# A leaky ReLU taken from SBUF instead of PSUM, and three buffers for the raw weights of a later layer, in a fused attention and mixture-of-experts kernel

## The chip, the cores and the metric

The kernel runs on one core of a Trainium2 chip. Its time is the device time of one execution in microseconds (us). Three runs of the kernel before took 1252.9, 1254.32 and 1254.36 us, so its time is the median, 1254.32 us. The engines are named as in the profile: PE is TensorE (PEld its weight loads), DVE is VectorE, ACT is ScalarE, POOL is GpSimd, and SP is SyncE, which issues most of the DMAs (SPq is its queue).

## The reference

Three layers follow one another; nothing goes back to the host in between.

```python
# 1. attention between x (8, 8, 512, 64) and a state (8, 8, 32, 64), both ways
a  = softmax(x @ state.T / 8);   xread = a  @ state
a2 = softmax(state @ x.T / 8);   sread = a2 @ x
x  = concat([xread, sread])                 # 8 * 544 = 4352 tokens of 512
# 2. a dense layer with a leaky ReLU
h = x @ w_in                                # 512 -> 2048
g = np.maximum(0.01 * h, h)
x = g @ w_out                               # 2048 -> 512
# 3. eight experts, one per token
e   = argmax(x @ w_gate)
out = gate_w * eom[e] * (np.maximum(x @ w1[e], 0) @ w2[e])   # w1: 512 x 1024, w2: 1024 x 512
```

## The kernel before

**Stages.** The kernel has two long phases. In the first, tokens go through attention and the dense layer in nine chunks: one for each batch element (512 tokens), and a last one of 256 tokens for `sread` of all of them. A chunk has 16 steps, one for each 128 columns of `w_in`. Step n runs `mm1(n)`, which makes `h` (128 x 512 in one PSUM bank), and two steps later (`DEPTH` is 2) `mm2(n)`, which multiplies the result with `w_out` into four other banks. In the second phase 37 slots of 128 tokens go through the experts.

**Precision.** Products that need fp32 accuracy are made of high and low parts: `gh` is u rounded to a shorter format (by ACT), `gl` is what is left (by DVE), and three matmuls stand for one.

**The activation, in `mm1`.** The bank `h` is read twice: ACT (L721) writes 0.01 * h into the SBUF tile `u`, and DVE (L722) takes the maximum of the bank and `u`. ACT then rounds `u` to `gh` (L197), and DVE subtracts (`gl`, L198, called in the next step before that step's `mm1`). The bank comes from the pool `psa`, which has four banks for everything but `mm2`: `h`, the bank `kps` in which k is made, the attention's banks, and the small sums `tot`.

**Work that runs beside the steps.** The lists of each engine are in the order of the program text, so a step's lines say what is queued behind what.

- In steps 0 to 14 `w_in` and `w_out` arrive as raw 64-bit numbers and are turned into fp32 (`from_double`): ACT L179 and L180, DVE L183 and L187, and POOL L190, and for `w_out` the split into `woh` (ACT L193) and `wol` (POOL L194). Tiles `wor` (raw `w_out`) come from the pool `ps_p`.
- From step 14 on, the generator `presplit` scales the experts' weights and splits them into two fp16 parts, in 32 jobs of two halves of 512 KB. A job has four parts, between its `yield`s: squares of half 0 (ACT L97), squares of half 1, then the sum over partitions on PE (`tot`, L139), the scale and `halve` of half 0, and last `halve` of half 1. `halve` is DVE L627 and L628 and POOL L629. SP writes each result to DRAM (L655, L636). One part runs in each step, and in chunk 7 from its third step on two parts, so that jobs 25 to 31 take two steps each.
- The raw halves come from the same pool `ps_p`, with two buffers. From job 25 on (`SPARE`), two of three jobs use the attention's tiles `x` and `xT` instead, which are free by then, and are loaded two jobs ahead (`ahead`).
- The attention of the next chunk and the router of the chunk before run one part in each step too.

Of the kernel before, what the change touches and what calls it, by code (L numbers as in the profile page):

```python
# [9 lines left out]
FP32 = mybir.dt.float32  # L10
FP32R = mybir.dt.float32r
# [3 lines left out]
ACTF = mybir.ActivationFunctionType  # L15
ALU = mybir.AluOpType
# [7 lines left out]
def tile_attention_moe_moe2(ctx, tc, x, state, w_in, w_out, w_gate, w_ogate, w1, w2, out):  # L24
    nc = tc.nc
    B, H, S, D = x.shape
    NS = state.shape[2]
    DM, FF = w_in.shape
    w_in, w_out = w_in.bitcast(I32), w_out.bitcast(I32)
    E, _, F2 = w1.shape  # L30
    NTOK = out.shape[0]
    TB = S + NS
    HP = H // 2
    G = 2
    R = S // 128
    KD = DM // 128
    NF = FF // 128
    KF = F2 // 128
# [4 lines left out]
    scale = 1.0 / float(D) ** 0.5  # L43
# [37 lines left out]
                                   op=ALU.arith_shift_right)  # L81
    nc.vector.tensor_copy(tqf, tq)
    for t in range(NSR // 128):
        nc.vector.scalar_tensor_tensor(out=toks[:, t:t + 1], in0=tqf, scalar=float(TB - NS),
                                       in1=pidx_f, op0=ALU.mult, op1=ALU.add)
        nc.vector.tensor_single_scalar(out=toks[:, t:t + 1], in_=toks[:, t:t + 1],
                                       scalar=float(t * (128 // NS) * TB + S), op=ALU.add)
# [5 lines left out]
    def squares(o, t):  # L93

        k, n = t.shape[1:]
        with nc.allow_low_precision(reason="of the sum only the exponent is used"):
            nc.scalar.activation(out=junk[:, 0:k * n].rearrange("p (k n) -> p k n", n=n), in_=t, func=ACTF.Square,  # L97
                                 scale=2.0 ** 0.5, accum_out=o)

    def norm_scale(pool, ss, s, inv):  # L100

        u = pool.tile(list(ss.shape), I32, tag=f"u{ss.shape[1]}", name="u")
        nc.vector.tensor_single_scalar(out=u, in_=ss.bitcast(I32), scalar=24, op=ALU.arith_shift_right)
        nc.vector.tensor_scalar(out=s.bitcast(I32), in0=u, scalar1=-float(1 << 23),
                                scalar2=float(205 << 23), op0=ALU.mult, op1=ALU.add)
        nc.vector.tensor_scalar(out=inv.bitcast(I32), in0=u, scalar1=float(1 << 23),
                                scalar2=float(49 << 23), op0=ALU.mult, op1=ALU.add)
# [27 lines left out]
    def over_partitions(*cols):  # L135

        ps = psa.tile([128, cols[0].shape[1]], FP32, tag="a", name="tot")
        for i, t in enumerate(cols):
            nc.tensor.matmul(ps, ones16.bitcast(BF16), t, start=(i == 0), stop=(i == len(cols) - 1))  # L139
        return ps  # L140
# [16 lines left out]
    x_p = ctx.enter_context(tc.tile_pool(name="x", bufs=1))  # L157
# [3 lines left out]
    ab = ExitStack()  # L161
# [3 lines left out]
    at1 = ab.enter_context(tc.tile_pool(name="at1", bufs=1))  # L165
# [30 lines left out]
    def split_later(h, l, t):  # L196
        nc.scalar.copy(out=h, in_=t)  # L197
        return lambda: nc.vector.tensor_tensor(out=l, in0=t, in1=h.bitcast(FP32), op=ALU.subtract)  # L198
# [189 lines left out]
    wo_p = ab.enter_context(tc.tile_pool(name="wo", bufs=1))  # L388
    k_p = ab.enter_context(tc.tile_pool(name="kp", bufs=2))
    g_p = ab.enter_context(tc.tile_pool(name="gp", bufs=2))  # L390
    ps_p = ab.enter_context(tc.tile_pool(name="pre", bufs=2))
    pq_p = ab.enter_context(tc.tile_pool(name="preq", bufs=2))

    woh = [wo_p.tile([128, DM], FP32R, name=f"woh{f}") for f in range(NF)]
# [13 lines left out]
    def stage_wi():  # L408
        i = len(wi_raw)
        if i < len(pieces):  # L410
            fc, kh = pieces[i]
            raw = r_p.tile([128, KD // 2, FC, 2], I32, tag="y", name="wir")
            nc.sync.dma_start(
                raw.rearrange("p k f t -> p k (f t)"),
                w_in[kh * 256:(kh + 1) * 256, 2 * fc * FC:2 * (fc + 1) * FC].rearrange("(k p) f -> p k f", p=128))
            wi_raw.append(raw)
# [175 lines left out]
    def presplit():  # L592

        jobs = [(e, half, m) for e in range(E) for half in range(2) for m in range(2)]

        SPARE = (NF * (B - 1) - NF + 2) // 4 + 1
        spare = {}

        def load(n, i):
            if n >= len(jobs) or (n, i) in spare:  # L600
                return spare.pop((n, i), None)
            e, half, m = jobs[n]
            k = (n - SPARE + 1) % 3 if n >= SPARE else 0
            shape = [128, KD, F2 // 4] if m == 0 else [128, KF // 4, DM]
            if k == 0:
                t = ps_p.tile(shape, FP32, tag="raw", name="raw")
            else:
                if i == 0:
                    room = x_p.tile([128, R, H, D], FP32, tag="x", name="x") if k == 1 else \
                        at1.tile([128, HP, R, 128], FP32, tag="xT", name="xT")  # L610
                    spare[n] = room.rearrange("p a b c -> p (a b c)").rearrange("p (i k f) -> p i k f", i=2, k=shape[1])
                t = spare[n][:, i]
            q = slice((2 * half + i) * 256, (2 * half + i + 1) * 256)
            if m == 0:
                nc.sync.dma_start(t, w1[e, :, q].rearrange("(k p) f -> p k f", p=128))
            else:
                nc.sync.dma_start(t, w2[e, q].rearrange("(k p) d -> p k d", p=128))
            return t

        def ahead(n):  # L620
            if n < len(jobs):
                t = load(n, 0), load(n, 1)
                spare[n, 0], spare[n, 1] = t

        def halve(t, s):
            pc = pq_p.tile([128, 2] + list(t.shape[1:]), FP16, tag="pc", name="pc")
            nc.vector.tensor_scalar(out=pc[:, 0], in0=t, scalar1=s, scalar2=None, op0=ALU.mult)  # L627
            nc.vector.tensor_scalar(out=t, in0=t, scalar1=s, scalar2=None, op0=ALU.mult)  # L628
            nc.gpsimd.tensor_tensor(out=pc[:, 1], in0=t, in1=pc[:, 0], op=ALU.subtract)  # L629
            return pc  # L630

        t0, last = load(0, 0), None
        for n, (e, half, m) in enumerate(jobs):
            wd = w1d if m == 0 else w2d
            if last is not None:
                nc.sync.dma_start(*last)  # L636
            t1 = load(n, 1)
            if n >= SPARE:
                ahead(n + 2)
            ss = sm.tile([128, 2], BF16, tag="ss2w", name="ss2w")  # L640
            squares(ss[:, 0:1], t0)
            yield
            squares(ss[:, 1:2], t1)
            yield
            sa = sm.tile([128, 1], FP32, tag="saw", name="saw")
            s = esc[:, m, half, e:e + 1]
            nc.vector.tensor_scalar(out=sa, in0=over_partitions(ss[:, 0:1], ss[:, 1:2]), scalar1=128.0, scalar2=2.0 ** -94,
                                    op0=ALU.mult, op1=ALU.max)
            norm_scale(sm, sa, s, einv[:, m, half, e:e + 1])
            pc = halve(t0, s)  # L650
            if n == SPARE - 1:
                ahead(n + 1)
                ahead(n + 2)
            yield
            nc.sync.dma_start(wd[e, :, 2 * half], pc)  # L655
            t0 = load(n + 1, 0)
            last = wd[e, :, 2 * half + 1], halve(t1, s)
            yield
        nc.sync.dma_start(*last)

# [22 lines left out]
    pre = presplit()  # L683
# [12 lines left out]
    DEPTH = 2  # L696
# [3 lines left out]
    def mm1(n):  # L700
        c, f, gi, i, gf = steps[n]
        kind, b = chunks[c]
        T = S if kind == "x" else NSR
        later = []
        if i == 0 and c > 0:
            if kind == "x" or f == 0:
                later.append(k_make(gi + 1))
            if kind == "s":
                later.append(k_make(gi + 2))
        mh, ml = (a1h[b], a1l[b]) if kind == "x" else (srh, srl)  # L710
        ps = psa.tile([128, T], FP32, tag="a", name="h")
        kt = KT[kind]
        sl = slice(i * 128, (i + 1) * 128)
        for k in range(kt):
            nc.tensor.matmul(ps, k_h[gi][:, k, sl], mh[k], start=(k == 0), stop=False)
            nc.tensor.matmul(ps, k_h[gi][:, k, sl], ml[k], start=False, stop=False)
            nc.tensor.matmul(ps, k_l[gi][:, k, sl], mh[k], start=False, stop=(k == kt - 1))  # L717
        if i == 1 and c == 0:
            later.append(k_make(gi + 1))
        u = g_p.tile([128, T], FP32, tag="u", name="u")  # L720
        nc.scalar.activation(out=u, in_=ps, func=ACTF.Copy, scale=0.01)  # L721
        nc.vector.tensor_tensor(out=u, in0=ps, in1=u, op=ALU.max)  # L722
        gh = g_p.tile([128, T], FP32R, tag="gh", name="gh", bufs=DEPTH + 1)
        gl = g_p.tile([128, T], FP32R, tag="gl", name="gl", bufs=DEPTH + 1)
        for f in later:
            f()
        gt[n] = (gh, gl)
        return lambda: split_later(gh, gl, u)
# [30 lines left out]
    load_x(0)  # L759
    for _ in range(2):  # L760
        stage_wi()
    for _ in range(2):
        stage_wo()
    g0 = attention(0)

# [28 lines left out]
    room = []  # L794
# [122 lines left out]
    for n in range(len(steps) + DEPTH):  # L917
        if n < len(steps):
            c, f = steps[n][0], steps[n][1]
# [168 lines left out]
```

## Time and profile before

| | |
|---|---|
| median of three runs | 1254.32 us |
| the profiled execution | 1242.63 us |
| its span, first to last instruction | 1240.9 us |
| chunk 0, 24.0 to 126.7 us | 102.7 us |
| chunks 2 to 6 | 87.9 us each |
| chunk 7, 655.3 to 750.7 us | 95.4 us |
| the experts, from 815 us | 425.9 us |
| DVE busy in the whole span | 788.4 us (64%) |

Busy times come from one execution, taken by the hardware profiler. Matmuls are pipelined and the end of each is modelled, so that PE can stand as busy while it waits a little. A group of instructions has its count, its busy time, the mean duration of one, and the idle time of its engine just before, with what ended it.

### The profile page before, as it was taken

Reading aid. Unit: us, or ns where it says so; the run is one execution under the profiler, and the core shown is the slowest. Engines: PE = TensorE matmul, PEld = TensorE weight load, DVE = VectorE, ACT = ScalarE, POOL = GpSimd, SP = SyncE. Lnnn points to the kernel's source line nnn. Section 1 sums busy time; section 2 is a strip of 40 time slices with the busy share of each in tenths; the row PEclk is TensorE's granted clock in tenths of the full one; section 3 lists DMA queues with packets and bytes.
Section 4 is the critical chain, followed back from the end, with each engine's and each line's share of the span. In section 5 each row is a group of like instructions: output and inputs, shape, how many; then the busy total and the mean of one; then the engine's idle time right before and its main releaser. Section 6 shows DMA issues by size and latency. Waiting matters only on the chain. (4 is left out here: it accounts for less than half of the span.)

```text
span 1240.9 us, 24399 instructions
## 1 busy us (share of the span) xinstructions
PE 1173.9 (95%) x9366; PEld 874.0 (70%) x9366; DVE 788.4 (64%) x1631; ACT 486.6 (39%) x950; POOL 380.4 (31%) x290
## 2 busy tenths in 40 slices
PE   5889999999999999999998887999999999999995
PEld 3557677777777777777776666877777777777773
DVE  6998786786786776786777888744643333333332
ACT  4876644544544545535444444321111111111111
POOL 3877224233323233232242353121211111111110
PEclk9899999999999999999998989999999999999998
DMA  5745346335445535445346732164216611133410
GB/s 164 223 154 136 107 119 170 99 111 170 132 119 146 154 106 165 112 129 151 95 145 187 212 135 87 52 204 166 74 52 240 260 53 44 44 128 111 182 50 23
DMA packets 133129, 161.65 MB, mean 130 GB/s; under 512 B 80015, under 2 KB 96399, under 8 KB 133008
## 3 DMA queue, kind: packets, MB, share of 16 engines
q1 hardware_dynamic: 124128, 131.65, 35.5%
q0 software_dynamic: 8880, 28.40, 6.6%
q8 instruction: 75, 1.23, 0.4%
q14 instruction: 46, 0.38, 0.1%
HBM read 229.71 MB, written 52.20 MB: 227 GB/s over the span
## 5 line engine op out<-in xcount | busy, mean ns | idle before, releaser
L739 PE MATMUL y<-woh,gh 128*128 128x512 f32 x544 | 227.7, 419 | 0.0
L741 PE MATMUL y<-woh,gl 128*128 128x512 f32 x544 | 217.3, 399 | 0.9 <-DVE gl L198 0.9
L740 PE MATMUL y<-wol,gh 128*128 128x512 f32 x544 | 217.0, 399 | 0.0
L629 POOL TENSOR_TENSOR pc<-raw,pc 128x1024 f16<-128x1024 f32 x54 | 128.0, 2370 | 248.7 <-issue 178.0
L1012 PE MATMUL h<-xt,w1t 128*128 128x128 f16 x1184 | 201.3, 220 | 0.0
L1013 PE MATMUL h<-xt,w1t 128*128 128x128 f16 x1184 | 201.2, 220 | 0.0
L1014 PE MATMUL h<-xt,w1t 128*128 128x128 f16 x1184 | 201.2, 219 | 0.0
L722 DVE TENSOR_TENSOR u<-h,u 128x512 f32<-128x512 f32 (+1 forms) x144 | 94.5, 657 | 114.7 <-ACT u L721 114.6
L1018 ACT ACTIVATE r<-h,room 128x512 f32<-128x512 f32 x74 | 50.8, 687 | 258.0 <-PE h L1014 258.0
L1020 DVE TENSOR_SCALAR rh<-h,room 128x512 f16<-128x512 f32 x74 | 55.5, 750 | 125.4 <-ACT r L1018 125.3
L1047 POOL DMA_INDIRECT out_dram<-osb,ti x37 | 37.5, 1014 | 310.9 <-DVE ti L1045 301.7
L197 ACT CAST gh<-u 128x512 fp32r<-128x512 f32 (+1 forms) x144 | 85.5, 594 | 109.0 <-DVE u L722 108.8
L739 PEld LDWEIGHTS y<-woh,gh 128*128 128x128 f32 x544 | 105.1, 193 | 31.9 <-issue 12.7
L741 PEld LDWEIGHTS y<-woh,gl 128*128 128x128 f32 x544 | 104.8, 193 | 25.6 <-DVE gl L198 1.3
L1012 PEld LDWEIGHTS <-w1t 128*128 128x128 f16 x1184 | 116.2, 98 | 4.7 <-issue 0.5
L1013 PEld LDWEIGHTS <-w1t 128*128 128x128 f16 x1184 | 116.2, 98 | 4.1
L740 PEld LDWEIGHTS y<-wol,gh 128*128 128x128 f32 x544 | 105.4, 194 | 18.8
L721 ACT ACTIVATE u<-h 128x512 f32<-128x512 f32 (+1 forms) x144 | 82.3, 572 | 88.4 <-PE h L717 86.9
L198 DVE TENSOR_TENSOR gl<-u,gh 128x512 fp32r<-128x512 f32 (+1 forms) x144 | 108.6, 754 | 12.1 <-ACT gh L197 10.3
L1014 PEld LDWEIGHTS <-w1t 128*128 128x128 f16 x1184 | 116.2, 98 | 0.0
L1037 PE MATMUL o<-w2t,rl 128*128 128x512 f16 x296 | 112.2, 379 | 0.1
L1035 PE MATMUL o<-w2t,rh 128*128 128x512 f16 x296 | 112.2, 379 | 0.1
(221 smaller groups left out, 2216.6 us busy)
## 6 DMA issues: line engine op xcount, KB each, us to landing
w1t<-w1s SPq DMA_DIRECT2D x152, 512.0 KB
w2t<-w2s SPq DMA_DIRECT2D x152, 512.0 KB
raw<-in_moe_w_dram SPq DMA_DIRECT2D x54, 512.0 KB
w1s<-pc SPq DMA_DIRECT2D x32, 512.0 KB
w2s<-pc SPq DMA_DIRECT2D x32, 512.0 KB
x<-in_x_dram SPq DMA_DIRECT2D x32, 256.0 KB
wir<-in_moe_w_in_dram SPq DMA_DIRECT2D x16, 512.0 KB
wor<-in_moe_w_out_dram SPq DMA_DIRECT2D x16, 512.0 KB
```

The costliest lines, as they stand in the source:

```text
L197: nc.scalar.copy(out=h, in_=t)
L198: return lambda: nc.vector.tensor_tensor(out=l, in0=t, in1=h.bitcast(FP32), op=ALU.subtract)
L629: nc.gpsimd.tensor_tensor(out=pc[:, 1], in0=t, in1=pc[:, 0], op=ALU.subtract)
L722: nc.vector.tensor_tensor(out=u, in0=ps, in1=u, op=ALU.max)
L739: nc.tensor.matmul(ys[c][t], gh[:, sl], woh[f], start=(f == 0), stop=False)
L740: nc.tensor.matmul(ys[c][t], gh[:, sl], wol[f], start=False, stop=False)
L741: nc.tensor.matmul(ys[c][t], gl[:, sl], woh[f], start=False, stop=(f == NF - 1))
L1012: nc.tensor.matmul(ps[:, i, :], wh, xt[:, k, :], start=(k == 0), stop=False)
L1013: nc.tensor.matmul(ps[:, i, :], wh, xt[:, KD + k, :], start=False, stop=False)
L1014: nc.tensor.matmul(ps[:, i, :], wl, xt[:, k, :], start=False, stop=(k == KD - 1))
L1035: nc.tensor.matmul(ps, h, w2t[q][:, 0, fi, :], start=(f == 0), stop=False)
L1037: nc.tensor.matmul(ps, l, w2t[q][:, 0, fi, :], start=False, stop=(f == KF - 1))
```

## The change

- L721 and L722: ACT copies the bank to `u` without a scale. DVE then takes the maximum of 0.01 * u and u, with one `scalar_tensor_tensor` whose two inputs are both the SBUF tile `u`. DVE doesn't read the bank.
- The pool `ps_p` has three buffers instead of two. At the start three raw pieces of `w_out` are loaded instead of two.
- `presplit` doesn't use `x` and `xT` any more. Half 0 of the next job is loaded at the start of a job, half 1 after `halve` of half 0; the load stands ahead of the write of the finished half.
- `gl` has two buffers instead of three.

```diff
-    ps_p = ab.enter_context(tc.tile_pool(name="pre", bufs=2))
+    ps_p = ab.enter_context(tc.tile_pool(name="pre", bufs=3))
...
-            if k == 0:
-                t = ps_p.tile(shape, FP32, tag="raw", name="raw")
-            else:
-                if i == 0:
-                    room = x_p.tile([128, R, H, D], FP32, tag="x", name="x") if k == 1 else \
-                        at1.tile([128, HP, R, 128], FP32, tag="xT", name="xT")
...
+            t = ps_p.tile([128, KD, F2 // 4] if m == 0 else [128, KF // 4, DM], FP32, tag="raw", name="raw")
...
-        t0, last = load(0, 0), None
+        t0, t1, last = load(0, 0), load(0, 1), None
         for n, (e, half, m) in enumerate(jobs):
             wd = w1d if m == 0 else w2d
+            next0 = load(n + 1, 0)
             if last is not None:
                 nc.sync.dma_start(*last)
-            t1 = load(n, 1)
-            if n >= SPARE:
-                ahead(n + 2)
...
-            if n == SPARE - 1:
-                ahead(n + 1)
-                ahead(n + 2)
             yield
+            next1 = load(n + 1, 1)
             nc.sync.dma_start(wd[e, :, 2 * half], pc)
-            t0 = load(n + 1, 0)
             last = wd[e, :, 2 * half + 1], halve(t1, s)
+            t0, t1 = next0, next1
...
-        nc.scalar.activation(out=u, in_=ps, func=ACTF.Copy, scale=0.01)
-        nc.vector.tensor_tensor(out=u, in0=ps, in1=u, op=ALU.max)
+        nc.scalar.copy(out=u, in_=ps)
+        nc.vector.scalar_tensor_tensor(out=u, in0=u, scalar=0.01, in1=u, op0=ALU.mult, op1=ALU.max)
...
-        gl = g_p.tile([128, T], FP32R, tag="gl", name="gl", bufs=DEPTH + 1)
+        gl = g_p.tile([128, T], FP32R, tag="gl", name="gl", bufs=DEPTH)
...
-    for _ in range(2):
+    for _ in range(3):
         stage_wo()
```

The order of DVE's list stays as it was. Here is a piece of it in a step of chunk 0, before: the two conversions of raw weights (L187), then `gl` of the last step, then the maximum `u`, and then `kl`, the low part of k.

```order
L183 TENSOR_SCALAR cv<-cv 128x512 x2
L187 SCALAR_TENSOR_TENSOR cv<-wir,cv 128x512
L187 SCALAR_TENSOR_TENSOR cv<-wor,cv 128x512
L198 TENSOR_TENSOR gl<-u,gh 128x512
L722 TENSOR_TENSOR u<-h,u 128x512
L198 TENSOR_TENSOR kl<-kps,kh 128x512
```

The same piece now:

```order
L183 TENSOR_SCALAR cv<-cv 128x512 x2
L187 SCALAR_TENSOR_TENSOR cv<-wir,cv 128x512
L187 SCALAR_TENSOR_TENSOR cv<-wor,cv 128x512
L198 TENSOR_TENSOR gl<-u,gh 128x512
L701 SCALAR_TENSOR_TENSOR u<-u 128x512
L198 TENSOR_TENSOR kl<-kps,kh 128x512
```

No row has moved; the row of `u` has another operation and reads no bank (`h` is gone from its inputs).

SP's list does move. In chunk 7, before, from the middle of job 26: `w1s` and `w2s` are the DRAM copies that are written, `yT` is a transpose of the router, and the loads go to the tiles `x`, `xT` and `raw`, both halves together.

```order
L655 DMA w2s<-pc 128x2048
L636 DMA w2s<-pc 128x2048
L615 DMA x<-in_moe_w_dram 128x4x256 x2
L514 DMA_TRANSPOSE yT<-row 128x8x128 x2
L655 DMA w1s<-pc 128x2048
L636 DMA w1s<-pc 128x2048
L617 DMA xT<-in_moe_w_dram 128x2x512 x2
L514 DMA_TRANSPOSE yT<-row 128x8x128
```

The same place now:

```order
L605 DMA raw<-in_moe_w_dram 128x2x512
L634 DMA w1s<-pc 128x2048
L603 DMA raw<-in_moe_w_dram 128x4x256
L620 DMA w1s<-pc 128x2048
L514 DMA_TRANSPOSE yT<-row 128x8x128
L603 DMA raw<-in_moe_w_dram 128x4x256
L634 DMA w2s<-pc 128x2048
L605 DMA raw<-in_moe_w_dram 128x2x512
L620 DMA w2s<-pc 128x2048
L514 DMA_TRANSPOSE yT<-row 128x8x128 x2
```

All loads go to `raw`. A load of one half now stands ahead of each write, and it is half 1 of the next job, or half 0 of the job after.

## Rows read from the trace of the kernel before

**Rows 1.** The page: each engine's busy time, share of the span, instructions

```profile
PE 1173.9 (95%) x9366; PEld 874.0 (70%) x9366; DVE 788.4 (64%) x1631; ACT 486.6 (39%) x950; POOL 380.4 (31%) x290
```

**Rows 2.** Busy time by stretch: chunk 0, chunk 2, chunk 7

```profile
24.00:126.70 102.70, 88.92 (x522) 63.48 (x520) 92.39 (x142) 73.29 (x143) 73.96 (x48) 0.93 0.57 165
...
215.70:303.60 87.90, 87.14 (x541) 64.54 (x539) 64.83 (x141) 43.80 (x89) 27.72 (x18) 1.00 0.47 134
...
655.30:750.70 95.40, 83.11 (x416) 62.41 (x415) 77.50 (x144) 45.81 (x86) 40.54 (x23) 0.91 0.54 175
```

**Rows 3.** PE's waits: line, what it waited for, us in total, times, longest

```profile
PE tot L139 <- ACT junk L97: 12.3, 8, 4.1
PE tot L139 <- DVE u L722: 5.6, 6, 1.8
```

**Rows 4.** DVE by line and shape, 31 to 124 us: busy, mean ns

```profile
L198 DVE TENSOR_TENSOR gl<-u,gh 128x512 fp32r<-128x512 f32 x14 | 21.1, 1508 | 0.0
L187 DVE SCALAR_TENSOR_TENSOR cv<-wor,cv 128x512 int32<-128x512 int32 x15 | 16.5, 1101 | 0.1
...
L722 DVE TENSOR_TENSOR u<-h,u 128x512 f32<-128x512 f32 x14 | 9.5, 679 | 0.7 <-ACT u L721 0.7
```

**Rows 5.** The same, 150 to 650 us

```profile
L198 DVE TENSOR_TENSOR gl<-u,gh 128x512 fp32r<-128x512 f32 x92 | 63.1, 686 | 7.5 <-ACT gh L197 5.8
```

**Rows 6.** Timeline of chunk 0 (start, duration): first and last overlap

```profile
29.27 1.59 POOL L190 TENSOR_TENSOR w<-cv,sign 128x512 f32<-128x512 f32 x1 [1.36 <-DVE cv L187]
29.66 0.68 DVE L722 TENSOR_TENSOR u<-h,u 128x512 f32<-128x512 f32 x1
...
119.42 1.68 POOL L190 TENSOR_TENSOR cv<-cv,sign 128x512 f32<-128x512 f32 x1 [2.37 <-DVE cv L187]
119.86 0.68 DVE L722 TENSOR_TENSOR u<-h,u 128x512 f32<-128x512 f32 x1
```

**Rows 7.** Timeline of chunk 0: where DVE sat idle (in brackets)

```profile
63.75 0.69 DVE L258 TENSOR_REDUCE mx<-bank 128x1 f32<-128x512 f32 x1 [1.14 <-ACT s L276]
70.53 0.69 DVE L258 TENSOR_REDUCE mx<-bank 128x1 f32<-128x512 f32 x1 [1.72 <-ACT s L276]
111.43 0.69 DVE L360 TENSOR_TENSOR a1l<-bank,a1h 128x512 fp32r<-128x512 f32 x1 [1.71 <-ACT a1h L359]
```

**Rows 8.** Timeline of chunk 7, the turn from one job to the next

```profile
693.63 0.68 DVE L198 TENSOR_TENSOR gl<-u,gh 128x512 fp32r<-128x512 f32 x1
693.85 2.48 POOL L629 TENSOR_TENSOR pc<-xT,pc 128x1024 f16<-128x1024 f32 x1 [1.47 <-issue]
694.24 0.68 DVE L722 TENSOR_TENSOR u<-h,u 128x512 f32<-128x512 f32 x1
...
697.86 0.16 PE L139 MATMUL tot<-ss2w,ones 128*128 128x1 bf16 x1 [0.56 <-ACT junk L97]
```

**Rows 9.** Timeline: a load and its first reader; a write and squares

```profile
648.58 0.39 SPq L615 DMA_DIRECT2D raw<-in_moe_w_dram  x1
...
655.21 1.06 ACT L97 ACTIVATE junk<-raw 128x1024 bf16<-128x1024 f32 x1 [1.52 <-DMA raw<-in_moe_w_dram]
...
743.19 0.33 SPq L655 DMA_DIRECT2D w1s<-pc  x1
...
746.66 1.06 ACT L97 ACTIVATE junk<-x 128x1024 bf16<-128x1024 f32 x1
```

**Rows 10.** Timeline of chunk 3: `gl`, the end of `mm2`, the next `u`

```profile
385.56 0.69 DVE L198 TENSOR_TENSOR gl<-u,gh 128x512 fp32r<-128x512 f32 x1
386.05 0.39 PE L741 MATMUL y<-woh,gl 128*128 128x512 f32 x1
...
388.52 0.69 DVE L722 TENSOR_TENSOR u<-h,u 128x512 f32<-128x512 f32 x1 [2.27 <-ACT u L721]
```

**Rows 11.** Timeline of chunk 4: ACT's and DVE's reading of one bank

```profile
393.19 0.60 ACT L721 ACTIVATE u<-h 128x512 f32<-128x512 f32 x1 [1.02 <-PE h L717]
...
393.81 0.69 DVE L722 TENSOR_TENSOR u<-h,u 128x512 f32<-128x512 f32 x1 [3.22 <-ACT u L721]
```

More of the change, by code (lines that the diff above doesn't have):

```diff
@@ L594, in presplit @@
         jobs = [(e, half, m) for e in range(E) for half in range(2) for m in range(2)]
-        SPARE = (NF * (B - 1) - NF + 2) // 4 + 1
-        spare = {}
         def load(n, i):
-            if n >= len(jobs) or (n, i) in spare:
-                return spare.pop((n, i), None)
+            if n >= len(jobs):
+                return None
             e, half, m = jobs[n]
-            k = (n - SPARE + 1) % 3 if n >= SPARE else 0
-            shape = [128, KD, F2 // 4] if m == 0 else [128, KF // 4, DM]
-            if k == 0:
-                t = ps_p.tile(shape, FP32, tag="raw", name="raw")
-            else:
-                if i == 0:
-                    room = x_p.tile([128, R, H, D], FP32, tag="x", name="x") if k == 1 else \
-                        at1.tile([128, HP, R, 128], FP32, tag="xT", name="xT")
-                    spare[n] = room.rearrange("p a b c -> p (a b c)").rearrange("p (i k f) -> p i k f", i=2, k=shape[1])
-                t = spare[n][:, i]
+            t = ps_p.tile([128, KD, F2 // 4] if m == 0 else [128, KF // 4, DM], FP32, tag="raw", name="raw")
             q = slice((2 * half + i) * 256, (2 * half + i + 1) * 256)
@@ L618, in load @@
             return t
[L620 to L623, printed above, removed]
         def halve(t, s):
@@ L646, in presplit @@
             s = esc[:, m, half, e:e + 1]
-            nc.vector.tensor_scalar(out=sa, in0=over_partitions(ss[:, 0:1], ss[:, 1:2]), scalar1=128.0, scalar2=2.0 ** -94,
-                                    op0=ALU.mult, op1=ALU.max)
+            nc.vector.tensor_scalar(out=sa, in0=over_partitions(ss[:, 0:1], ss[:, 1:2]), scalar1=128.0,
+                                    scalar2=2.0 ** -94, op0=ALU.mult, op1=ALU.max)
             norm_scale(sm, sa, s, einv[:, m, half, e:e + 1])
             pc = halve(t0, s)
-            if n == SPARE - 1:
-                ahead(n + 1)
-                ahead(n + 2)
             yield
+            next1 = load(n + 1, 1)
             nc.sync.dma_start(wd[e, :, 2 * half], pc)
-            t0 = load(n + 1, 0)
             last = wd[e, :, 2 * half + 1], halve(t1, s)
+            t0, t1 = next0, next1
             yield
```

## The prediction

> **What bounds the kernel now.** I read the page first. PE is busy for 95% of the span and no other engine for more than 64% [rows 1], so a faster activation is worth nothing by itself; what counts is where PE waits. So next came the busy times by stretch [rows 2]. Chunk 2 lasts 87.9 us with PE busy for 87.1; chunks 3 to 6 last the same to 0.1 us. There PE sets the pace. Two chunks differ. Chunk 0 lasts 102.7 us: PE is busy for 88.9, and DVE for 92.4, 90% of it, as DVE and POOL convert the raw weights there. Chunk 7 has no attention to make for a next chunk, fewer matmuls (416 against 541), and still lasts 95.4 us: PE idles for 12.3 us, and its granted clock is 0.91, where chunk 2 has 1.00. PE's list of waits says why [rows 3]: `tot`, the sum over partitions in `presplit`, waited 12.3 us for ACT's squares, all eight times in chunk 7. So in these two chunks, some 200 us, the chain through DVE, POOL and ACT sets the time; elsewhere PE does.
>
> The third view is DVE by line in chunk 0 [rows 4]. Two of its operations have the same size: `gl` subtracts one SBUF tile from another and takes 1508 ns, and `u` takes the maximum of a PSUM bank and an SBUF tile in 679 ns. In the middle chunks, where POOL does little, `gl` takes 686 ns [rows 5]. The timeline shows that `gl` is long in chunk 0 because it stands behind a running POOL operation until that has ended, while `u` runs in 0.68 us though a POOL multiplication has been going on for 0.4 us already [rows 6]. So in this trace a DVE operation with two SBUF inputs waits for POOL's running operation, and one with a PSUM input doesn't. The change turns the second kind into the first, 144 times.
>
> **The maximum from SBUF.** Uncovered by POOL, it costs what `gl` costs, 686 ns [rows 5] against 679 now [rows 4]: nothing. [...] ACT's copy without a scale is the same operation as with it: nothing.
>
> What it costs under POOL I count in the timeline. *Chunk 0:* each of the first 15 `u` starts while a POOL multiplication runs that has 1.2 us still to run (0.49 once). The first starts at 29.66 with the POOL operation ending at 30.86, the last at 119.86 with the end at 121.10 [rows 6]. Summed over the 15, this is 17.7 us of blocking. Not all of it counts. Behind the 6th, 7th and 13th `u`, DVE idles for 1.14, 1.72 and 1.71 us, for ACT [rows 7], which waits there for POOL and PE and not for `u`; these three blocks are hidden, and those of the last two steps fall where PE sets the pace again. Ten others remain in full at 1.2 us less one idle stretch of 0.7, and one of 0.49: 11 us. A shift also takes other operations out of a POOL operation or into one: L187 takes 1101 ns in the mean [rows 4], about 0.42 us over the 0.68 of one that is not blocked, 6.3 us in 15 steps that the shift may free. I take +10, with +4 (11 less all of that) and +16 (nearly all of the 17.7) as bounds. PE cannot make this up later, since it has no idle time in chunks 2 to 6 in which to catch up.
>
> *Chunk 7:* here the chain from one `tot` to the next counts. At the turn of a job, `gl` runs at 693.63, POOL's subtraction L629 begins at 693.85 and runs to 696.33, and `u` begins at 694.24 beside it [rows 8]. Then come `gh` on ACT, both squares behind `gh` in ACT's list, and `tot` at 697.86, for which PE waits. With two SBUF inputs `u` stands behind L629 until 696.33, 2.1 us, and `gh`, the squares and `tot` are late by as much. The same pattern gives 1.5, 2.1, 2.1 and 1.3 us for jobs 26 to 29; in the other turns no L629 runs under `u`, or it isn't on the chain. Sum: +7, with bounds of +3 and +10.
>
> *Middle chunks:* five `u` in each stand behind L629, for 6 to 7 us per chunk. DVE has 23 us idle in a chunk [rows 2], and `gh` and `gl` are needed by `mm2` two steps, some 11 us, later; the longest block is 2.1 us. Nothing, as long as no bank that PE waits for comes late.
>
> **The bank is free earlier.** PE waited six times, 5.6 us together, for a bank that DVE's `u` still read [rows 3], once in each of chunks 1 to 6. ACT is done with such a bank at 393.79, DVE at 394.50 [rows 11]: each wait shrinks by 0.7 us. -4.2; the bounds are -5.6 and, if a late `u` holds back other banks, +2.
>
> **Buffers and loads.** In chunks 1 to 6 a job has four steps, some 22 us, and half 1 is now loaded two steps ahead of its squares instead of one: hidden before, hidden after. In chunk 7 the spare tiles with their two jobs of lead are gone. Half 1 of the next job goes where half 0 was, so SP issues its load when L629 of half 0 has ended, which is when the write of half 0 is issued now (L655). The 19 loads for which ACT waited took 4.3 us or more from their issue to the reader's start, the last of them 6.6, from 648.58 to 655.21 [rows 9]. The time at hand, from L655 to the squares of half 1, is 3.5 us in the last job (743.19 to 746.66) [rows 9], 4.3 us in two others, and 5.6 or more in the rest. In those with the least, but the last, the blocked `u` gives some 1.3 to 2 us more. So the last job is late by 1 to 3 us and one or two others by up to 1. +1.5, bounds 0 and +5. ACT, which waits for the load, has the next copy of `h` queued behind.
>
> Two buffers for `gl`: DVE's write of `gl(n)` must now wait for the end of `mm2(n-2)`. In 13 of 144 steps it starts up to 0.88 us before that: 385.56, where the last matmul ends at 386.44 [rows 10]. The next in DVE's list is `u` of the next step, at 388.52, which waits for a product that PE makes after that `mm2`. 386.44 and 0.69 is 387.13: hidden. The third raw piece of `w_out` is issued third in its row at the start, behind all that is needed first: nothing.
>
> **Sum.** 10 + 7 + 1.5 - 4.2 = +14.3 us on the profiled execution of 1242.6 us, so 1256.9. The timed runs lie at 1254.3, 11.7 us above that execution; the sum goes on top of the median: 1268.6, say 1268 us. The bounds added up give +1 to +33.
>
> **Rivals.**
>
> 1. *No block, since both inputs are one tile.* All blocked operations in this trace read two different tiles; none reads the same one twice, so the rows can't exclude that the second input comes for free. Then the bank's gain stays, -4.2, with the late loads at +1.5: 1251.6, faster by 0.2%. It decides if `u` keeps 0.68 us in chunk 0. Against it: L187 is the same operation, with two SBUF tiles, and its 1101 ns [rows 4] have the block in them. [...] 11%.
> 2. *Blocked, but hidden.* The earlier bank lets PE run ahead in chunks 0 and 7, so that ACT's data come earlier, and the shift frees L187: +4 and +3, 0 for loads, -4.2, together +3 and 1257 us, at the limit of what can be told. 14%.
> 3. *The loads set the pace of chunk 7.* If each of seven jobs waits for its half 1, with 6.6 us and the write beside it, each is late by some 2 us more: 1268 + 12 = 1280 us. For it: the traffic is uneven in chunk 7; against it: the blocked `u` gives the loads time. 17%.
>
> **How the numbers follow.** The forecast has 58%, the rivals 11, 14 and 17. A measurement of this kernel can tell 0.2%, 2.5 us, from no change. Faster: rival 1 and little else, of which a part lies within the limit, 0.10. Same: the rest of it and a third of rival 2, 0.10. Slower: 0.80. The range goes from 1253, within rival 2's low end, to 1281, rival 3.
>
> **What would show it.** In chunk 0 `u` should take 1.6 to 1.9 us in the mean, chunk 0 should last 109 to 118 us, and `gl` stay near 1.5. In chunk 7 `u` should be at 2 us or more where it follows `gl` and L629, and PE's wait for ACT's squares should grow from 12.3 to about 20 us; an entry for ACT's squares waiting for `raw` should stand near the end of the chunk. Chunks 2 to 6 should last 87.2 us and the six waits for DVE's `u` be gone. If `u` stays at 0.7 us, the mechanism is wrong; if it is long and chunk 0 keeps its 102.7 us, the chain is.

## The result and the profile after

The changed kernel takes 1271.76 us (median of 4 runs, 1270.91 to 1272.22); the kernel before, timed beside it, 1254.17 us (1252.90 to 1254.36). The ratio is 1.0142, with a 95% interval of 1.0124 to 1.0159: slower by 17.6 us, inside the forecast range and 3.8 us above the forecast.

The two profiled executions differ by more, 1272.22 against 1242.63 us. So I cut both spans by the same borders, the first matmul of each chunk's first product and the first of the experts:

| stage, us | before | after | difference |
|---|---|---|---|
| ahead of chunk 0 | 24.0 | 23.6 | -0.4 |
| chunk 0 | 102.6 | 109.4 | +6.8 |
| chunk 1 | 89.0 | 89.5 | +0.5 |
| chunks 2 to 6, each | 87.9 | 88.7 | +0.8 |
| chunk 7 | 95.5 | 105.9 | +10.4 |
| chunk 8 | 66.9 | 63.6 | -3.3 |
| experts | 423.3 | 434.8 | +11.5 |

Up to the experts the difference is 18.1 us (835.7 against 817.6), which is what the timed runs show. The +11.5 of the experts, whose code is unchanged, is no part of it, as the repeated runs below show.

The same three stretches as in [rows 2], and then chunk 8, from the profile after (start:end, length, busy time of PE, weight load, DVE, ACT, POOL with instructions, granted clock, DMA share, GB/s):

```profile
23.60:133.00 109.40, 91.59 (x522) 64.69 (x520) 104.99 (x142) 73.37 (x144) 72.03 (x48) 0.89 0.52 156
222.50:311.20 88.70, 87.38 (x541) 64.32 (x539) 71.81 (x141) 42.12 (x87) 27.41 (x18) 1.00 0.47 132
666.10:772.00 105.90, 85.20 (x416) 63.95 (x415) 85.68 (x146) 44.50 (x84) 41.38 (x24) 0.92 0.51 154
772.00:835.70 63.70, 55.68 (x384) 48.20 (x384) 44.60 (x135) 23.05 (x58) 15.25 (x18) 0.97 0.36 116
```

DVE works 12.6 us longer in chunk 0 with the same 142 instructions, 7.0 us longer in chunk 2 and 8.2 us in chunk 7. In chunk 2 PE now idles for 1.3 us, where it idled for 0.8.

PE's waits after, to be held against [rows 3] (line, what it waited for, us in total, times, longest):

```profile
PE tot L139 <- ACT junk L97: 20.7, 12, 3.3
PE h L696 <- DVE kl L198: 9.8, 4, 5.3
PE bank L355 <- DVE rc L309: 7.9, 6, 1.3
```

The wait for ACT's squares has grown from 12.3 to 20.7 us. The six waits of `tot` for DVE's `u`, 5.6 us, are gone, and six others stand there, 7.9 us, for a bank of the attention (L355). The wait for `kl` lies in chunk 0, where `kl` stands behind `u` in DVE's list; before, it was half as long:

```profile
PE h L717 <- DVE kl L198: 4.8, 2, 4.0
```

PE is idle for 4.0 us more in chunk 0 than before. The rest of the 6.8 us, some 2.7, is busy time of PE, whose mean granted clock there is 0.89 where it was 0.93.

DVE by line and shape, 31 to 124 us, which answers to [rows 4]:

```profile
L701 DVE SCALAR_TENSOR_TENSOR u<-u 128x512 f32<-128x512 f32 x13 | 22.6, 1738 | 0.3 <-ACT u L700 0.3
L198 DVE TENSOR_TENSOR gl<-u,gh 128x512 fp32r<-128x512 f32 x13 | 20.4, 1568 | 0.0
L187 DVE SCALAR_TENSOR_TENSOR cv<-wor,cv 128x512 int32<-128x512 int32 x13 | 9.9, 764 | 0.0
```

And from 150 to 650 us, as [rows 5]:

```profile
L701 DVE SCALAR_TENSOR_TENSOR u<-u 128x512 f32<-128x512 f32 x91 | 103.5, 1138 | 53.2 <-ACT u L700 52.4
L198 DVE TENSOR_TENSOR gl<-u,gh 128x512 fp32r<-128x512 f32 x91 | 62.4, 686 | 11.7 <-PE y L720 7.0 <-ACT gh L197 3.2
```

`u` has gone from 679 to 1738 ns in chunk 0, and L187 from 1101 to 764: the shift frees it of most of its own block. (`gl` has the same 21.8 us in the whole of chunk 0 before and after; its higher mean here comes from the 13 steps that fall into this stretch.) The timeline near the start of chunk 0 answers to [rows 6]:

```profile
28.79 1.59 POOL L190 TENSOR_TENSOR w<-cv,sign 128x512 f32<-128x512 f32 x1 [1.37 <-DVE cv L187]
29.17 1.75 DVE L701 SCALAR_TENSOR_TENSOR u<-u 128x512 f32<-128x512 f32 x1
```

POOL ends at 30.38 and `u` at 30.92, 0.54 later: it ends behind POOL's operation, where the one of [rows 6] ran beside it. The same in chunk 7, where POOL's subtraction (L629, now L612) takes 2.46 us, to be held against [rows 8]:

```profile
719.38 0.69 DVE L198 TENSOR_TENSOR gl<-u,gh 128x512 fp32r<-128x512 f32 x1
719.61 2.46 POOL L612 TENSOR_TENSOR pc<-raw,pc 128x1024 f16<-128x1024 f32 x1 [1.47 <-issue]
719.99 2.63 DVE L701 SCALAR_TENSOR_TENSOR u<-u 128x512 f32<-128x512 f32 x1
```

The new wait at L355 is in the middle chunks. One place of chunk 3, first before, then after (start, duration, engine, line; in brackets the idle time ahead):

```profile
364.07 2.47 POOL L629 TENSOR_TENSOR pc<-raw,pc 128x1024 f16<-128x1024 f32 x1 [0.68 <-POOL xT L334]
...
364.46 0.68 DVE L722 TENSOR_TENSOR u<-h,u 128x512 f32<-128x512 f32 x1
365.06 0.67 DVE L198 TENSOR_TENSOR kl<-kps,kh 128x512 fp32r<-128x512 f32 x1
365.66 0.14 DVE L309 TENSOR_SCALAR rc<-su 128x1 f32<-128x1 f32 x1
...
366.69 0.60 PE L355 MATMUL bank<-id,xT 128*128 128x128 f32 x4
```

```profile
371.36 2.47 POOL L612 TENSOR_TENSOR pc<-raw,pc 128x1024 f16<-128x1024 f32 x1 [0.69 <-POOL xT L334]
371.75 2.63 DVE L701 SCALAR_TENSOR_TENSOR u<-u 128x512 f32<-128x512 f32 x1
...
374.30 0.68 DVE L198 TENSOR_TENSOR kl<-kps,kh 128x512 fp32r<-128x512 f32 x1
374.90 0.14 DVE L309 TENSOR_SCALAR rc<-su 128x1 f32<-128x1 f32 x1
...
375.13 0.63 PE L355 MATMUL bank<-id,xT 128*128 128x128 f32 x4 [1.30 <-DVE rc L309]
```

Before, `kl` and `rc` were done 0.9 us ahead of the transposes of L355. After, both stand in DVE's list behind a `u` of 2.63 us, and PE idles for 1.30 us until they are done. This happens once in each of chunks 1 to 6.

One `u` is blocked for longer than one POOL operation. It is the last long one of chunk 7; first the place before, then after:

```profile
744.24 0.68 DVE L722 TENSOR_TENSOR u<-h,u 128x512 f32<-128x512 f32 x1
744.60 2.17 POOL L629 TENSOR_TENSOR pc<-raw,pc 128x1024 f16<-128x1024 f32 x1
```

```profile
759.63 1.26 POOL L587 DMA_INDIRECT srt<-row,posi  x1 [0.16 <-issue]
760.54 4.32 DVE L701 SCALAR_TENSOR_TENSOR u<-u 128x512 f32<-128x512 f32 x1
760.90 2.17 POOL L612 TENSOR_TENSOR pc<-raw,pc 128x1024 f16<-128x1024 f32 x1
763.00 1.30 POOL L194 TENSOR_TENSOR kl<-w,kh 128x512 fp32r<-128x512 f32 x1
```

After, `u` begins 0.36 us ahead of L612 and still ends at 764.86, 0.56 us after L194: it has stood behind two POOL operations in a row.

### The profile page after: what moved, and what is told of

It is laid out like the page before. It is cut to its first block, busy times and chain, and to the rows that moved or that the text cites. A ratio compares the mean times of both kernels' runs of the same rounds, so it can differ in the third digit from the quotient of the medians.

```text
span 1270.5 us, 24417 instructions
## 1 busy us (share of the span) xinstructions
PE 1186.4 (93%) x9366; PEld 871.3 (69%) x9366; DVE 847.1 (67%) x1631; ACT 481.0 (38%) x950; POOL 378.5 (30%) x290
## 5 line engine op out<-in xcount | busy, mean ns | idle before, releaser
L612 POOL TENSOR_TENSOR pc<-raw,pc 128x1024 f16<-128x1024 f32 x64 | 151.9, 2373 | 284.7 <-DVE raw L611 186.3
L701 DVE SCALAR_TENSOR_TENSOR u<-u 128x512 f32<-128x512 f32 (+1 forms) x144 | 168.3, 1169 | 73.5 <-ACT u L700 71.2
L719 PEld LDWEIGHTS y<-wol,gh 128*128 128x128 f32 x544 | 105.9, 195 | 19.0
L198 DVE TENSOR_TENSOR gl<-u,gh 128x512 fp32r<-128x512 f32 (+1 forms) x144 | 106.0, 736 | 17.5 <-PE y L720 9.6
L696 PE MATMUL h<-a1h,kl 128*128 128x512 f32 x256 | 102.6, 401 | 11.6 <-DVE kl L198 9.8
```

The lines of the kernel that those rows point to most:

```text
L701: nc.vector.scalar_tensor_tensor(out=u, in0=u, scalar=0.01, in1=u, op0=ALU.mult, op1=ALU.max)
L719: nc.tensor.matmul(ys[c][t], gh[:, sl], wol[f], start=False, stop=False)
```

## The experiments

The theory: `u` stands behind POOL's running operation since both inputs lie in SBUF, and that lengthens chunks 0 and 7 and, by the bank of L355, the middle ones. The rivals: the buffers and later loads cost the time; or the longer `u` is a matter of the operation and not of POOL. Times are compared with the kernel before side by side on the same chip.

**Before, once more, unchanged.**

> The kernel before, unchanged, profiled once more, since its first profiled execution (1242.6 us) lies 11.7 us under its timed runs. Both theories expect about 1253 us now, with chunk 0 at 102.7 us, chunks 2 to 6 at 87.9 us and chunk 7 at 95.4 us as before, and the 11 us more in the experts' phase. If they lie in the first phase instead, the comparison by chunk has to be made anew.

One time, 1236.6 us, below what was expected; 23 timed runs of the kernel before on this chip have a median of 1240.09 (1235.87 to 1244.31). Chunk 0 lasts 102.2 us, chunks 2 to 6 87.9, the experts 422.3. Chunk 7 lasts 91.4 where the first profile had 95.5, so that chunk alone tells nothing below some 4 us. The times in the next three expectations start from 1254 us as well and are missed by as much; what counts there is the ratio.

**The buffers alone.** The changed kernel with the activation of before:

```diff
-nc.scalar.copy(out=u, in_=ps)
-nc.vector.scalar_tensor_tensor(out=u, in0=u, scalar=0.01, in1=u, op0=ALU.mult, op1=ALU.max)
+nc.scalar.activation(out=u, in_=ps, func=ACTF.Copy, scale=0.01)
+nc.vector.tensor_tensor(out=u, in0=ps, in1=u, op=ALU.max)
```

> The changed buffers and loads, with the old activation (the maximum reads the bank). Theory of the block (the cost comes from the maximum with two SBUF inputs, which waits for POOL): 1252 to 1257 us, chunk 0 at 102 to 103 us, chunks 2 to 6 at 87.9 us, chunks 7 and 8 together at most 3 us longer than before, the late loads. Rival (the lost lead of the loads sets the pace of chunk 7): chunk 7 at 103 us or more, 1260 to 1264 us, and ACT's squares waiting for raw in several jobs.

1241.45 us, 1.0014 of before (0.9997 to 1.0030): no difference that can be told. Chunk 0 lasts 103.0, chunks 2 to 6 87.9, chunk 7 96.7, chunk 8 63.5. PE's waits:

```profile
PE tot L139 <- ACT junk L97: 13.4, 8, 4.1
PE tot L139 <- DVE u L701: 5.7, 6, 2.0
```

They are those of [rows 3] to 1.1 us. Buffers and loads are not where the 17.6 us went.

**The activation alone.** The same four lines the other way round, in the kernel before:

> The new activation, with the old buffers, loads and depth of gl. Theory of the block: 1267 to 1273 us, nearly all of the change's loss, with chunk 0 at 108 to 110 us, u at 1.6 to 1.8 us there, each of chunks 2 to 6 at 88.7 us, chunk 7 at 100 us or more. Rival of the loads: 1258 to 1264 us, chunk 7 near 95 us.

1260.54 us, 1.0164 (1.0139 to 1.0189): the whole change. Chunks 0, 2 and 7:

```profile
23.60:133.70 110.10, 91.61 (x522) 65.12 (x520) 104.06 (x142) 73.97 (x146) 72.57 (x48) 0.88 0.52 155
222.70:311.40 88.70, 87.39 (x540) 64.33 (x538) 71.77 (x141) 42.83 (x88) 27.59 (x18) 1.00 0.48 133
666.20:772.80 106.60, 86.69 (x416) 64.69 (x415) 85.35 (x146) 45.05 (x86) 41.36 (x24) 0.89 0.48 157
```

and PE's waits:

```profile
PE tot L139 <- ACT junk L97: 19.9, 12, 4.0
...
PE bank L355 <- DVE rc L309: 7.8, 6, 1.4
```

Both new waits are there without the other parts of the change. Its chunks 7 and 8 together take 169.8 us; 169.5 in the changed kernel.

**The same operation, one input from the bank.** In the changed kernel:

```diff
-nc.vector.scalar_tensor_tensor(out=u, in0=u, scalar=0.01, in1=u, op0=ALU.mult, op1=ALU.max)
+nc.vector.scalar_tensor_tensor(out=u, in0=u, scalar=0.01, in1=ps, op0=ALU.mult, op1=ALU.max)
```

> The changed kernel with one operand other: the second input of the maximum is the PSUM bank and not u; operation, scalar, ACT's copy, buffers and loads stay. Theory of the block: u back at 0.68 us in chunk 0, and the whole time within 0.2% of the run with the changed buffers alone (1252 to 1257 us). Rival (the operation itself, or ACT's copy, is dearer than the old pair): u longer than 0.8 us in every chunk, and 1265 us or more.

1240.86 us, 1.0006 (0.9992 to 1.0019): as fast as before, by one operand. DVE from 31 to 124 us, and PE's waits:

```profile
L198 DVE TENSOR_TENSOR gl<-u,gh 128x512 fp32r<-128x512 f32 x15 | 21.8, 1452 | 0.0
L187 DVE SCALAR_TENSOR_TENSOR cv<-wor,cv 128x512 int32<-128x512 int32 x15 | 16.5, 1102 | 0.1
L701 DVE SCALAR_TENSOR_TENSOR u<-u,h 128x512 f32<-128x512 f32 x15 | 10.2, 677 | 0.4 <-ACT u L700 0.3
```

```profile
PE tot L139 <- ACT junk L97: 12.8, 8, 4.1
PE tot L139 <- DVE u L701: 5.6, 6, 1.9
```

`u` takes 677 ns, L187 is back at 1102, and the waits for `u` are back. So it is neither the operation nor ACT's copy; it is where the second input lies. In the changed kernel the two SBUF inputs are one and the same tile, and it is blocked all the same: 1738 ns in the mean from 31 to 124 us, against 677 with the bank as the second input.

**POOL's subtraction (L612) on DVE.** In the changed kernel:

```diff
-nc.gpsimd.tensor_tensor(out=pc[:, 1], in0=t, in1=pc[:, 0], op=ALU.subtract)
+nc.vector.tensor_tensor(out=pc[:, 1], in0=t, in1=pc[:, 0], op=ALU.subtract)
```

> The changed kernel with POOL's subtraction of presplit (L612) on DVE instead, so that POOL has no long operation on SBUF in chunks 2 to 6 but the attention's L334. Theory of the block: u falls from about 1150 ns to 700 to 800 ns in chunks 1 to 6; if nothing else comes in its place, the wait for rc goes and the earlier bank counts, so that chunks 2 to 6 take 87.2 to 87.9 us instead of 88.7; chunk 0 stays at 109 us, since its POOL operations are others; chunk 7 may go either way, as DVE gets some 17 us of work there. Rival (u is slow for another reason than POOL): u stays above 1 us in chunks 1 to 6.

1261.32 us, 1.0071 (1.0047 to 1.0096), so half of the loss is gone. `u`, from 150 to 650 us:

```profile
L701 DVE SCALAR_TENSOR_TENSOR u<-u 128x512 f32<-128x512 f32 x91 | 62.7, 689 | 56.0 <-ACT u L700 55.2
```

With L612 gone from POOL, the 91 `u` of the middle fall from 1138 to 689 ns, chunk 7 lasts 97.5 instead of 105.9, and the wait at L355 is gone. Chunk 0, where the blocking operation is L190, keeps its 109.4, and `u` there its 1741 ns. The middle chunks take 88.2, above the 87.2 to 87.9 expected: in each, PE waits some 0.2 us for `gl` and 0.3 for a bank that ACT's copy still reads (L292), and its busy time is 87.65 us, 0.5 more than in the first-step version below, which takes 87.2. Where those 0.5 come from isn't shown.

**Only the steps that gain.** In the kernel before, the maximum from SBUF in the first step of chunks 1 to 8 alone:

```diff
+if f == 0 and c > 0:
+    nc.scalar.copy(out=u, in_=ps)
+    nc.vector.scalar_tensor_tensor(out=u, in0=u, scalar=0.01, in1=u, op0=ALU.mult, op1=ALU.max)
+else:
     nc.scalar.activation(out=u, in_=ps, func=ACTF.Copy, scale=0.01)
     nc.vector.tensor_tensor(out=u, in0=ps, in1=u, op=ALU.max)
```

> The kernel before, with the new maximum from SBUF in the first step of each chunk from 1 on alone; there tot waits for the bank, and the trace of before has no POOL operation under u. Theory (two effects of the new maximum, the earlier bank for good, the block for bad): the six waits for DVE's u go, chunks 1 to 6 take 87.2 us, 4 to 5 us less in all, ratio 0.996 to 0.998. Rival (the earlier bank gives nothing that lasts): 87.9 us and no change.

1250.04 us, 0.9971 (0.9953 to 0.9988). Chunk 2:

```profile
216.00:303.20 87.20, 87.18 (x541) 64.53 (x539) 65.24 (x141) 43.48 (x89) 27.55 (x18) 1.00 0.48 135
```

PE has no idle time left in it, and the six waits for `u` are gone. The gain of the earlier bank is real, 0.7 us a chunk, and needs one step in sixteen; the other fifteen bring the loss.

**`gl` two deep, alone.** In the kernel before:

```diff
-gl = g_p.tile([128, T], FP32R, tag="gl", name="gl", bufs=DEPTH + 1)
+gl = g_p.tile([128, T], FP32R, tag="gl", name="gl", bufs=DEPTH)
```

> The kernel before with two buffers for gl instead of three, and nothing else. Both theories expect no change within 0.2%, each chunk within 0.3 us of before; DVE's gl starts up to 0.9 us later in about 13 steps, and the next u at the same time as before. If it is slower by 0.3% or more, the depth of gl has a part in the change's loss.

1254.39 us, 1.0000 (0.9981 to 1.0019): nothing, as the prediction had it. By chunk the 0.3 us isn't kept: chunk 1 lasts 91.0 us, where it had 89.0 and 89.6 in the two profiles of the kernel before.

**The changed kernel, once more.**

> The changed kernel once more, timed on the same chip as the others. Theory of the block: ratio 1.013 to 1.017, chunk 0 at 109 to 110 us, chunks 2 to 6 at 88.7 us, chunks 7 and 8 together 5 to 8 us longer than before. The experts' phase, 434.8 us in its first profile, is to be 422 to 423 us here, as in all other runs, or else the change makes that phase slower by a way that no theory has.

1271.80 us, 1.0158 (1.0132 to 1.0184). Chunk 0 lasts 111.5, above the 109 to 110 expected, chunks 2 to 6 88.7, chunk 7 105.9, chunk 8 62.2. The experts last 435.9, where 422 to 423 had been expected: my guess that a repeat would show the short experts was wrong. But the two versions above that are built on the kernel before have 435.4 and 436.0 on the same chip, so the level isn't the change's.

**The other way round: `gl` from the bank in chunk 0.** On top of the first-step version, chunk 0 writes the maximum back into the bank, so that `gh` and `gl` read it there and `gl` has one SBUF input:

```diff
+    if c == 0:
+        nc.vector.tensor_tensor(out=ps, in0=ps, in1=u, op=ALU.max)
+        u = ps
+    else:
         nc.vector.tensor_tensor(out=u, in0=ps, in1=u, op=ALU.max)
```

> The kernel of e5, and in chunk 0 the maximum is written back into its PSUM bank, so that ACT rounds gh from the bank and gl has one PSUM and one SBUF input. Theory of the block: gl falls from 1508 ns to about 0.69 us in chunk 0, DVE has some 11 us less to do there, and chunk 0 takes 95 to 100 us instead of 102.5; ratio to before 0.990 to 0.995. Rival (the bank, now held until gl in the next step, is missed by PE): gl as short, but chunk 0 at 103 us or more, PE waiting for banks that gl reads.

1242.29 us against 1250.96 of before beside it, 0.9928 (0.9906 to 0.9950). DVE from 31 to 124 us:

```profile
L187 DVE SCALAR_TENSOR_TENSOR cv<-wor,cv 128x512 int32<-128x512 int32 x15 | 17.6, 1176 | 0.1
L727 DVE TENSOR_TENSOR h<-h,u 128x512 f32<-128x512 f32 x16 | 11.0, 689 | 3.0 <-ACT u L725 3.0
L198 DVE TENSOR_TENSOR gl<-h,gh 128x512 fp32r<-128x512 f32 x16 | 10.9, 682 | 0.6 <-ACT gh L197 0.6
```

`gl` has fallen from 1508 [rows 4] to 682 ns, and chunk 0 lasts 98.8 us where the first-step version had 102.4. It is the change read backwards: one SBUF input fewer in the step that POOL covers.

**The same in chunk 7 too** (`c == 0 or c == B - 1`).

> As e8, and in chunk 7 too. In chunk 7 gl mostly runs ahead of POOL's subtraction and is blocked in few steps (702 ns in the mean before), so the theory of the block expects chunk 7 within 1.5 us of e8's; the rival (banks) expects chunk 7 longer by 2 us or more, since tot needs a bank there twice as often.

1240.29 us, 0.9915 (0.9892 to 0.9938), the best of all. Chunk 7:

```profile
647.40:738.30 90.90, 80.91 (x416) 60.72 (x415) 72.70 (x144) 45.20 (x86) 38.63 (x23) 0.96 0.59 187
```

It lasts 90.9 us, 4.9 below the version before this one and so outside the 1.5 expected; yet the unchanged kernel had 91.4 once, and the intervals of the two versions overlap. That chunk 7 gains is not shown; that the version beats both kernels is.

## Why the prediction was right, and which steps failed

*The block of `u`, and chunk 0.* Right in kind, too large by a third: +6.8 where +10 stood. (Chunk 0 lasts 109.4 to 111.5 us in the four profiles with the new activation in all steps, 102.2 to 103.0 with a bank as one input.) DVE's rows for the whole of chunk 0, two before and the same two after:

```profile
L187 DVE SCALAR_TENSOR_TENSOR cv<-wor,cv 128x512 int32<-128x512 int32 x16 | 17.2, 1075 | 0.1
L183 DVE TENSOR_SCALAR cv<-cv 128x512 int32<-128x512 int32 x30 | 16.8, 595 | 0.0
```

```profile
L183 DVE TENSOR_SCALAR cv<-cv 128x512 int32<-128x512 int32 x30 | 19.1, 672 | 0.0
L187 DVE SCALAR_TENSOR_TENSOR cv<-wor,cv 128x512 int32<-128x512 int32 x16 | 12.0, 749 | 0.1
```

The sixteen `u` take 16.9 us more (forecast 17.7 for fifteen). L187 takes 6.3 less, 5.2 of them in the rows shown and 1.1 for `w_in`; L183 takes 2.3 more, 672 ns in the mean for 595, as the shift brings more of it under POOL; one small operation on `gsa` takes 1.0 less; `gl` is unchanged. That makes +11.9 of the +12.6 us by which DVE is busier. DVE's idle time in the chunk fell from 10.3 to 4.4 us, so 5.9 us lay where it idled anyway, and +6.8 was left. The step that was mis-sized is the choice of +10 between +4 and +16: I had worked out that the shift may free 6.3 us of L187, and counted about 1 of it; all 6.3 were freed, and 2.3 came back at L183. The sum has a slip as well: ten blocks of 1.2 us less 0.7, and one of 0.49, make 11.8 and not 11.

*The lock of chunk 7.* Right in kind, with one block missed. From the chunk's start to its last long `u` the way is 5.5 us longer than before (94.4 against 88.9): that is what came of the turns that I had counted at +7, where `u` takes 1.9 to 2.6 us. From that `u` to the end of the chunk it is 4.9 us longer, and 3.6 of them are the `u` of 4.32 us, where it took 0.68. For this turn I had nothing, as no L629 ran yet when `u` began. PE's wait for the squares is 20.7 us, against "about 20", with 4.0 of it in this turn. The chunk is longer by 10.4 us, but chunk 8 is shorter by 3.3, for a reason that isn't shown: +7.1 for the two, against +7 for the lock and +1.5 for the loads. That this term fits is in part luck. The effect itself is well clear of what the chunk varies by: 105.9 to 106.6 us in three profiles, against 91.4 to 96.7 with the maximum from the bank.

*The middle chunks: the step that failed.* The prediction put them at nothing, "as long as no bank that PE waits for comes late", and took -4.2 for the earlier bank, with 87.2 us a chunk. A bank does come late. I had followed `u` only to its own readers, `gh` and `gl`, which have 11 us; behind `u` in DVE's list stand `kl` and `rc`, for which the transposes of L355 wait, with 0.9 us to spare. The bank's gain is there (first-step version: 87.2), and 1.3 us come back at L355, most of what makes 88.7 of 87.2. Over chunks 1 to 6 the two terms together are +4.5 (4.0 of them in chunks 2 to 6) where -4.2 stood; the bound of +2 that I gave to a late `u` that holds back other banks was less than half of it.

*The loads and the buffers.* The forecast of +1.5 has nothing behind it. In the changed kernel no wait of ACT for `raw` stands in the stretch 660 to 780 us, where an entry was foretold. With the activation of before, 0.7 us of such a wait appears, once; that fits the prediction's remark that the blocked `u` gives the loads time, but doesn't prove it. The buffers alone are 1.0014, and with the new activation they add nothing (1.0142 and 1.0158 with them, 1.0164 without). `gl` two deep costs nothing. The third raw piece of `w_out` was not tried by itself. ACT's copy without a scale takes 582 ns in the mean, against 595 with it: nothing, as foretold. (The waits of ACT for loads that the prediction counts as 19 are 18 in the profile's list.)

*The sum.* Forecast 10 - 4.2 + 7 + 1.5 = 14.3; measured 6.8 + 4.5 + 7.1 - 0.4 (the start) = 18.0. The total came close by luck: -3.2 in chunk 0, -1.4 in chunks 7 and 8 and -0.4 at the start stand against +8.7 in the middle. What the prediction had right is the mechanism, the block of `u`, and the two chunks that it lengthens most.

*The rivals.* That one tile as both inputs isn't blocked (1251.6) falls with `u` at 1738 ns. That the block is hidden (1257) falls in chunks 0 and 7, though a third of chunk 0's block was hidden. That the loads set the pace of chunk 7 (1280) falls with the missing wait. Where no block is in the way, the move from the bank is worth nothing, as foretold: `u` takes 689 ns from SBUF (150 to 650 us, with the subtraction on DVE) and 677 to 688 with the bank as one input.

*Blocked with one tile.* Rival 1 says that all blocked operations of the trace before read two different tiles. They don't. L628 scales the tile `raw` in place, with one number for each partition as its other operand. It takes 0.75 us free, and beside POOL, in the trace before:

```profile
740.63 2.53 POOL L629 TENSOR_TENSOR pc<-raw,pc 128x1024 f16<-128x1024 f32 x1 [6.04 <-issue]
741.18 2.53 DVE L628 TENSOR_SCALAR raw<-raw,esc 128x1024 f32<-128x1024 f32 x1
```

It ends 0.55 us after POOL's operation. L183, with one tile and a constant, takes 0.42 us in the median and up to 1.56. So for `u` and `gl` a second SBUF input is enough for a block, as the experiments show (677 against 1738 ns, and 682 against 1508), but it isn't needed by every operation; what L183 and L628 wait for was not tested.

## What to carry to other kernels

Before an input is moved from PSUM to SBUF to free a bank, count the SBUF inputs of each DVE operation that runs beside POOL: for the maximum and the subtraction here the second one cost the rest of POOL's operation (677 ns became 1738 for the maximum in chunk 0, and `gl` had 1508 where one input fewer gave 682), once even of two in a row (4.32 us), and the better direction was to leave a value in the bank (0.9928 of before, against 1.0142). One input alone is no safe sign, as L183 and L628 show (up to 1.56 us for 0.42, and 2.53 for 0.75). For such a block, follow not only the readers of the delayed tile but everything queued behind it on its engine, and hold each against the slack of the one that waits for it. Take the gain where it is: one step in sixteen had it (0.9971), and the other fifteen brought only a price.

## What the runs showed that was not expected

The experts' phase, whose code is the same in all kernels here, has a length that goes with the chip, or with the sitting, as each chip was used in one, and not with the kernel. On one chip it lasted 422.3 to 423.2 us in four kernels (the kernel before timed at 1240.09), on a second 435.2 to 436.0 in four others (before: 1253.03), on a third 432.1 and 432.3 (before: 1250.96). That would also explain why the first profile of the kernel before, with experts of 423.3, lay 11.7 us below its timed runs; on which chip it ran is not recorded, so this isn't shown. Two profiles are compared stage by stage, and a stage that neither kernel touches shows how far that is needed.
